# Linear attention and a bilinear FFN on one core: regrouped units, one more group by seven products, every step placed by a plan

## The chip, the core and the metric

The kernel runs on one core of a Trainium2 chip. The engines named here are TensorE (PE, matmuls; PEld its weight loads), VectorE (DVE), ScalarE (ACT), GpSimd (POOL) and SyncE (SP, which issues nearly all DMAs). Each takes its own instructions in order and waits on semaphores for the others. The metric is device microseconds of one execution, the median of several runs.

## The reference

q, k and v are (4 batches, 8 heads, 768 positions, 64), float32. The attention is linear with a decay lam per head. The result is transposed to x, 3,072 rows of 512, and goes through a bilinear FFN: w_a and w_b are 512 x 1,536, w_out is 1,536 x 512.

```python
for b in range(nb):
    intra = np.einsum('bhic,bhjc->bhij', qb, kb) * Dmask[None]
    intra = np.einsum('bhij,bhjd->bhid', intra, vb)
    inter = np.einsum('bhid,bhde->bhie', qb * lam_pow[None], kv_state)
    out[:, :, sl] = intra + inter
    kv_state = lam_block[None, :, None, None] * kv_state + np.einsum('bhsd,bhse->bhde', kb_dec, vb)
a = x @ w_a
b = x @ w_b
return (a * b @ w_out).astype(np.float32)
```

## The kernel before

Work is cut into 24 units: four batches of six blocks of 128 positions, all heads. `GROUPS` (line 28) joins units into groups of 4, 1, 2, 4, 4, 4, 4 and 1; the FFN runs on a group at a time, while the attention of later units is put between its matmuls.

Steps of one unit: q, k and v are loaded as float32 (`load_x`, line 181), q and k are scaled by powers of lam to bf16 (`make_ks`, `make_qs`, lines 406 and 411), v is cast (`make_vb`, 414), q and k are transposed (a DMA for units in `DMA_T`, else `piece_T` on TensorE, 438), scores are made (`scores`, 451, half the array at a time) and masked (`mask`, 465), the state is updated (`kv_update`, `kv_beside`, `kv_copy`, 535 to 560), and `pieces_O` (571) makes inter and intra products and evacuates them to xT. The first four units are loaded and transposed together (lines 336 to 352 and 874 to 1000).

The FFN of a group: `ffn` (646) makes a and b by plain matmuls over 512, multiplies them to ab and multiplies ab by w_out. The groups in `Z_GROUPS` (82) make a and b by `ffn_z` (714): the two-by-two block product is made by seven block products instead of eight (Strassen's scheme), from sums of weights (`weight_sum`, 260) and of xT (`x_sums`, 700). Each of the six column pairs n of ffn_z makes tiles U, V and W in PSUM, ScalarE snapshots (`snap`, 809), VectorE subtracts them into oab, a ring of two buffers, and multiplies oab to ab (line 738). Groups in `ZO_GROUPS` (83) do the product with w_out in seven products too: `ab_sum` (814) makes sums of ab, and `out_half` (835) runs 14 halves, placed into the next group. The other groups' out stage is plain.

What sets the order is written out in the source. `PLAN` (line 42) lists for each group pairs of slot and piece; the FFN functions call `hook(slot)` after each step, and the hook emits the pieces of that slot. Each engine then has the order of emission as its queue. Which engine takes a piece is in tables (`MASK_ACT`, `KV_ENG`, `VB_ENG`, `SUM_ENG`, `XS_ENG`, `WS_ENG`, `WO_ENG`, lines 87 to 110). Loads are not in the plan: `pump` (302) issues the next ones of a fixed list whenever a piece has freed a place, with all weights ahead of units 4 and later. The products of oab to ab are always VectorE's and come right behind the last of the seven products.

```python
    for g, n in enumerate(GROUPS):
        if g in Z_GROUPS:
            ffn_z(g, g_u0[g], gx.pop(g), hook, joined, own)
        else:
            ffn(g_u0[g], n, gx.pop(g), hook, g == 0, g + 1 == len(GROUPS))
```

Of the kernel before, what the change touches and what calls it, by code (L numbers as in the profile page):

```python
# [16 lines left out]
F32 = mybir.dt.float32  # L17
# [5 lines left out]
def _bc(ap, dims):  # L23
# [4 lines left out]
GROUPS = (4, 1, 2, 4, 4, 4, 4, 1)  # L28
W_CHUNKS = (256,) * 6
W_STEPS = ((0, 1), (2,), (3,), (4, 5))  # L30
W_HALVES = (4, 5)
LOOKAHEAD = {9: 2, 10: 1}
DMA_T = range(7, 24)
KEEP_GROUPS = 2
PACK = 4

PLAN = {
# [38 lines left out]
}  # L81
Z_GROUPS = (3, 4, 5, 6)
ZO_GROUPS = (4, 5, 6)
FIN_AT = 5
N_LATE = 3
# [28 lines left out]
def kernel(  # L114
# [116 lines left out]
    def cast_w(kind, c, eng):  # L231
        t, slot = staged.pop((kind, c))
        if slot is not once:
            slots.append(slot)
# [844 lines left out]
```

## Time and profile before

| what | value |
|---|---|
| median of 3 runs | 225.31 us (225.09 to 227.28) |
| span of the profiled execution | 224.7 us |
| granted TensorE clock | 1.000 over the span |
| TensorE busy | 214.6 us, 2,235 matmuls |
| VectorE busy | 164.8 us, 269 instructions |
| ScalarE busy | 123.2 us, 251 instructions |
| GpSimd busy | 101.1 us, 95 instructions |
| moved by DMA | 39.42 MB, mean 175 GB/s |

The profile is of one execution; its span goes from the first to the last instruction of the kernel. Busy time of an engine is the union of its instructions' times. A matmul's duration holds its way through the array, so neighbours overlap, and the rate of a stream is read from start to start, not from the mean duration. A name such as L730 is a line of the kernel; `op out<-in` names the tiles. "Idle before, releaser" is what an engine waited for.

### The profile page before, as it was taken

To read this page: it belongs to the slowest core of one execution; us is meant where nothing else is said; L and a number is where in the kernel's file an instruction comes from. 1 tells how busy PE (TensorE), PEld (TensorE's weight loads), DVE (VectorE), ACT (ScalarE), POOL (GpSimd) and SP (SyncE) were. 2 spreads that over 40 slices of the span, in tenths; PEclk is the share of its full clock that TensorE was granted. 3 is DMA by queue.
4 is the path that set the end of the run, shared out by engine and by line. 5 is a ranking of instruction groups with operands and counts; after the bars stand their busy time and mean duration, and the time that the engine had idled before them with its cause. 6 is when DMAs were issued, how large, how long until landed. Compare 5 with 4: busy or idle time off the path is not lost.

```text
span 224.7 us, 5609 instructions
## 1 busy us (share of the span) xinstructions
PE 214.6 (96%) x2235; PEld 158.8 (71%) x2235; DVE 164.8 (73%) x269; ACT 123.2 (55%) x251; POOL 101.1 (45%) x95
## 2 busy tenths in 40 slices
PE   7699999989989999999999999899999999999994
PEld 2375444437768757887547878688888888887994
DVE  1895673599699659989878999968686765777440
ACT  3586446017544247775366988776536665533322
POOL 6061004256895075541459359786417722052000
PEclk9999999999999999999999999999999999999999
DMA  4999999998999999999999999652021100112042
GB/s 137 316 231 356 356 384 346 276 217 192 229 198 218 219 180 240 204 253 247 175 240 243 243 206 202 138 98 48 2 88 55 50 1 4 47 48 95 0 143 93
DMA packets 99081, 39.42 MB, mean 175 GB/s; under 512 B 85488, under 2 KB 95088, under 8 KB 99056
## 3 DMA queue, kind: packets, MB, share of 16 engines
q1 hardware_dynamic: 98768, 39.00, 78.0%
q8 instruction: 17, 0.28, 0.5%
q10 hardware_dynamic: 288, 0.07, 0.1%
q14 instruction: 8, 0.07, 0.1%
HBM read 28.32 MB, written 6.29 MB: 154 GB/s over the span
## 4 chain that ended last, share of the span: by engine, by line
PE 80%; DVE 6%; DMA 6%; ACT 3%; issue 2%; SPq 1%; ACTq 0%; DVEq 0%
PE U L730 17%; PE op L852 12%; PE b_ps L596 9%; PE op L643 8%; PE V L730 8%; PE a_ps L596 8%; PE op L792 5%; PE W L730 4%; DMA wst<-in_moe_w_b_dram 4%; PE o_ps L497 3%; DMA k<-in_k_dram 3%; PE kq L457 2%; PE kvd L527 1%; SPq L350 1%; DVE m L480 1%
## 5 line engine op out<-in xcount | busy, mean ns | idle before, releaser
L811 ACT COPY u<-U 128x512 f32<-128x512 f32 x48 | 28.4, 591 | 16.9 <-PE U L730 16.6
L401 POOL TENSOR_TENSOR qk<-kf,lp_k 128x512 bf16<-128x512 f32 x18 | 19.8, 1099 | 34.6 <-DMA kf<-in_k_dram 23.1
L623 DVE TENSOR_TENSOR ab<-a_sb,b_ps 128x128 bf16<-128x128 bf16 (+2 forms) x48 | 19.2, 417 | 14.0 <-ACT a_sb L605 11.1
L480 DVE TENSOR_TENSOR m<-kq,lotri 128x512 bf16<-128x512 f32 x40 | 25.7, 684 | 3.8 <-PE kq L457 3.6
L596 PE MATMUL a_ps<-xT,wa_sb 128*128 128x128 bf16 (+2 forms) x200 | 27.8, 268 | 0.6 <-ACT xT L520 0.5
L596 PE MATMUL b_ps<-xT,wb_sb 128*128 128x128 bf16 (+2 forms) x192 | 27.5, 272 | 0.7 <-ACT oab L736 0.5
L738 DVE TENSOR_TENSOR ab<-oab 128x1024 bf16<-128x1024 bf16 x24 | 18.4, 767 | 10.5 <-ACT oab L736 10.5
L401 POOL TENSOR_TENSOR qk<-qf,lp_q 128x512 bf16<-128x512 f32 x20 | 25.2, 1259 | 1.2 <-DMA qf<-in_q_dram 1.2
L605 ACT CAST a_sb<-a_ps 128x128 bf16<-128x128 f32 (+2 forms) x48 | 17.1, 375 | 14.4 <-PE a_ps L596 14.3
L643 PE MATMUL op<-wo_sb,ab 128*128 128x512 bf16 (+2 forms) x120 | 22.8, 337 | 0.2 <-DVE wo_sb L254 0.2
L596 PEld LDWEIGHTS <-wa_sb 128*128 128x128 bf16 x200 | 16.6, 98 | 6.6 <-issue 0.7
L596 PEld LDWEIGHTS <-wb_sb 128*128 128x128 bf16 x192 | 15.7, 98 | 7.3 <-DVE wb_sb L251 0.7
L730 PEld LDWEIGHTS <-wz_a 128*128 128x128 bf16 x192 | 18.2, 98 | 3.6 <-issue 0.7
L730 PEld LDWEIGHTS <-wz_b 128*128 128x128 bf16 x192 | 18.7, 98 | 2.2
L730 PE MATMUL U<-xT,wz_a 128*128 128x256 bf16 x96 | 18.3, 272 | 0.0
L730 PE MATMUL U<-xT,wz_b 128*128 128x256 bf16 x96 | 18.3, 272 | 0.0
L520 ACT CAST xT<-o_ps 128x512 bf16<-128x512 f32 (+1 forms) x24 | 12.2, 556 | 10.7 <-PE o_ps L497 10.5
L420 POOL CAST vb<-vf 128x512 bf16<-128x512 f32 x14 | 10.9, 778 | 13.9 <-DMA vf<-in_v_dram 13.9
L769 DVE TENSOR_TENSOR oab<-U,u 128x512 bf16<-128x512 f32 x24 | 16.4, 682 | 0.4 <-PE U L730 0.4
L730 PEld LDWEIGHTS <-wa_sb 128*128 128x128 bf16 x144 | 13.4, 97 | 4.5 <-issue 1.7
L643 PEld LDWEIGHTS <-ab 128*128 128x128 bf16 x120 | 10.1, 98 | 8.6 <-issue 0.3
L736 ACT CAST oab<-U 128x512 bf16<-128x512 f32 x24 | 14.2, 591 | 3.6 <-PE U L730 3.5
(126 smaller groups left out, 453.8 us busy)
## 6 DMA issues: line engine op xcount, KB each, us to landing
vf<-in_v_dram SPq DMA_DIRECT2D x24, 256.0 KB, 4.8
qf<-in_q_dram SPq DMA_DIRECT2D x20, 256.0 KB, 4.6
kf<-in_k_dram SPq DMA_DIRECT2D x20, 256.0 KB, 4.6
out_dram<-o_sb SPq DMA_DIRECT2D x18, 256.0 KB, 2.5
wst<-in_moe_w_a_dram SPq DMA_DIRECT2D x6, 512.0 KB, 8.5
wst<-in_moe_w_b_dram SPq DMA_DIRECT2D x6, 512.0 KB, 9.0
wst<-in_moe_w_out_dram SPq DMA_DIRECT2D x6, 512.0 KB, 10.6
out_dram<-o_kept SPq DMA_DIRECT2D x5, 256.0 KB, 4.4
```

Source lines behind the costliest of these rows:

```text
L401: eng_of(eng).tensor_mul(dst.rearrange("p (c b) d -> p b c d", b=2), x[:].rearrange("p (b c) d -> p b c d", b=2), lp.rearrange("p (b c) o ...
L480: nc.vector.tensor_mul(m, kq[i], lotri_bc)
L596: nc.tensor.matmul(ps[:, lo:hi], lhsT=w_sb[:, s, f * 128:(f + 1) * 128], rhs=xT[:, s, lo:hi], start=(s == 0), stop=(s == KS - 1), skip_gro ...
L605: nc.scalar.copy(a_sb[:, :gt], ps[:, :gt])
L623: nc.vector.tensor_mul(ab[:, f, :gt], a_sb[:, :gt], ps[:, :gt])
L643: nc.tensor.matmul(op[:, lo:hi], lhsT=ab[:, f, t * 128:(t + 1) * 128], rhs=wo_sb[:, f, lo:hi], start=(f == 0), stop=(f == FC - 1))
L730: nc.tensor.matmul(ps[:, k, :], lhsT=wt[:, s, n * 128:(n + 1) * 128], rhs=rhs[i][:, s, :], start=(fresh and k == 0 and s == 0), stop=True, ...
L736: nc.scalar.copy(oab[:, 0], U)
L738: nc.vector.tensor_mul(ab[:].rearrange("p (h i) (t c) -> p h i t c", h=2, t=2)[:, :, n], o5[:, :, :, 0, :], o5[:, :, :, 1, :])
L769: nc.vector.tensor_sub(oab[:, 1], U, v1)
L811: nc.scalar.copy(t, ps)
L852: nc.tensor.matmul(ps[:, t, :], lhsT=lhs[p][:, n, t * 128:(t + 1) * 128], rhs=rhs[:, n, :], start=fresh, stop=True, skip_group_check=True)
```

## The change

The groups become 4, 1, 3, 4, 4, 4, 4. The group of three also goes by seven products, with tiles of 192 columns (hw, half a group's columns, in place of the fixed 256); its out stage is plain. The four groups of four all have their out stage by seven products. The plan now holds every step after the first scaling of q and k: loads (LQ, LK, LV, LW), casts of parts of a weight (CW), scaling (PK, PQ), casts of v (CV), transposes (TR), scores (S), masks (M), state (V, K), outputs of attention and their evacuation (O, E), sums (X, WS, WO, SM), out halves (H), products of oab (MU) and late stores (W). A table VAR names for each step which engine or form it takes. `pump` and its look-ahead are gone. All tiles that are loaded are float32, as before.

Three forms are new. Scores may be made in 64 x 64 quarters of the array, 16 matmuls instead of 8 (VAR of S); inter may use all 128 rows (VAR of O); products of oab may run on GpSimd (VAR of MU), which 13 of 30 do. Masks of a unit lie in one tile, so that one VectorE operation can mask both halves. The rows of the first four units that are kept for later stores lie in other tiles. In the built program TensorE has 2,327 matmuls instead of 2,235 and changes between whole, half and quarter array 87 times instead of 81; 16 transposes go by DMA instead of 17.

```diff
-GROUPS = (4, 1, 2, 4, 4, 4, 4, 1)
+GROUPS = (4, 1, 3, 4, 4, 4, 4)
+Z_GROUPS = (2, 3, 4, 5, 6)
+ZO_GROUPS = (3, 4, 5, 6)
...
 PLAN = {
...
+    5: [
+        (-1, 'X', (5, 1)), (-1, 'H', (3, 9)), (-1, 'PK', 22), (-1, 'LV', 21), (-1, 'V', 20),
+        (1, 'SM', (4, 0)), (1, 'SM', (4, 2)), (2, 'H', (3, 12)), (2, 'LQ', 22), (2, 'LV', 23),
...
+VAR = {('CV', 3): 2,
...
+  ('MU', (6, 0)): 1,
+  ('MU', (6, 1)): 1,
+  ('O', (5, 6)): 1,
+  ('PK', 4): 1,
...
+    def dve_pool(name, arg):
+        return nc.gpsimd if var(name, arg) else nc.vector
...
     def scores(u, kq=None):
         d = U[u]
         kq = kq or score_banks()
+        step = 64 if var("S", u) else 128
         for hp in range(HP):
-            for i in range(2):
-                p = slice(64 * i, 64 * i + 64)
-                nc.tensor.matmul(kq[i][:, hp, :], lhsT=d["kT"][p, hp, :], rhs=d["qT"][p, hp, :],
-                                 start=True, stop=True, skip_group_check=True)
+            for j in range(0, 128, step):
+                for i in range(2):
+                    p, r = slice(64 * i, 64 * i + 64), slice(j, j + step)
+                    nc.tensor.matmul(kq[i][r, hp, :], lhsT=d["kT"][p, hp, r], rhs=d["qT"][p, hp, :],
+                                     start=True, stop=True, skip_group_check=True)
...
+    def times(x):
+        g, n = x
+        hw = outs[g]["hw"]
+        o5 = oabs[x][:].rearrange("p (h t) k c -> p h t k c", h=2)
+        dve_pool("MU", x).tensor_mul(
+            outs[g]["ab"][:].rearrange("p (h i) x -> p h i x", h=2)[:, :, n, :2 * hw]
+            .rearrange("p h (t c) -> p h t c", t=2),
+            o5[:, :, :, 0, :], o5[:, :, :, 1, :])
...
         def last_product(n, U, oab):
             product(U, n, 2)
             nc.scalar.copy(oab[:, 0], U)
-            o5 = oab[:].rearrange("p (h t) k c -> p h t k c", h=2)
-            nc.vector.tensor_mul(
-                ab[:].rearrange("p (h i) (t c) -> p h i t c", h=2, t=2)[:, :, n],
-                o5[:, :, :, 0, :], o5[:, :, :, 1, :])
+            oabs[g, n] = oab
...
+        last = g + 1 == len(GROUPS) and i == 13
...
+        if last:
+            for t in range(T):
+                o = o_pool.tile([128, 256], F32, name="o_end", tag="osb")
+                nc.scalar.copy(o, ps[:, t, :])
+                (nc.scalar if t else nc.sync).dma_start(out=out_r[d["u0"] + t, :, :HN], in_=o)
+            return
...
+        hook, plan = hooks(g)
+        hook(-1)
         if g in Z_GROUPS:
-            bank["held"] = set(range(5))
-            joined = any(name == "H" and us[0] < g for slot, name, us in PLAN[g])
-            own = any(slot >= 18 for slot, name, us in PLAN[g])
-            ffn_z(g, g_u0[g], gx.pop(g), hook, joined, own)
+            hold(5)
+            ffn_z(g, g_u0[g], gx[g], hook, g - 1 in ZO_GROUPS,
+                  g not in ZO_GROUPS or g + 1 == len(GROUPS))
+        elif g:
+            hold(0)
+            ffn_plain(g_u0[g], n, gx[g], hook)
         else:
-            bank["held"] = {3, 4} if fin else set()
-            if fin:
-                fin.pop()()
-            ffn(g_u0[g], n, gx.pop(g), hook, g == 0, g + 1 == len(GROUPS))
+            ffn(g_u0[g], n, hook)
```

`ffn_plain` is the plain FFN of the group of one unit, with four column blocks to a PSUM tile; `plain_out` is a plain out stage that runs all units' early matmuls first and the last ones behind them.

More of the change, by code (lines that the diff above doesn't have):

```diff
@@ new lines, in dma_T, with make_vb @@
+    def dma_T(u):
+        qkT = qkT_pool.tile([128, 2, HP, 128], BF16, name="qkT", tag="qkT")
+        nc.sync.dma_start_transpose(
+            out=qkT[:].rearrange("p j hp i -> p (j hp) i"),
+            in_=U[u]["qk"][:].rearrange("p j h d -> p (j h d)"))
+        U[u]["qT"], U[u]["kT"] = qkT[:, 0], qkT[:, 1]
+    def make_vb(u):
+        vb = prep_pool.tile([128, H, D], BF16, name="vb", tag="vb", bufs=N_VB)
+        how = var("CV", u)
+        if how == 2:
+            nc.scalar.copy(vb, raw[u, "v"])
+        else:
+            (nc.vector if how else nc.gpsimd).tensor_copy(vb, raw[u, "v"])
+        raw[u, "v"] = vb
@@ L646, in ffn, with ffn_first @@
-    def ffn(u0, n, xT, hook, first, last):
+            nc.tensor.matmul(op, lhsT=ab[:, f, t * 128:(t + 1) * 128],
+                             rhs=wo_sb[:, f, :], start=(f == f0), stop=(f == f1))
+    f_ps, f_a = {}, {}
+    f_ab = []
+    def ffn_first(x):
+        kind, f, part = x
+        gt = n0 * BLK
+        lo, hi = ((0, gt // 2), (gt // 2, gt), (0, gt))[part]
+        ps_parts[0] = part < 2
+        k = kind, f
+        f_ps[k] = half(wa_sb if kind == "a" else wb_sb, f, gx[0], kind + "_ps", lo, hi, f_ps.get(k),
+                       {("a", 0): 0, ("a", 1): 3, ("b", 0): 4, ("b", 1): 5}[k] if part == 0 else None)
+        ps_parts[0] = False
+        if part == 0:
+            return
+        if kind == "a":
+            f_a[f] = a_copy(f_ps[k], gt)
+        else:
+            if not f_ab:
+                f_ab.append(ab_pool.tile([128, FC, 512], BF16, name="ab", tag="ab"))
+            nc.vector.tensor_mul(f_ab[0][:, f, :gt], f_a[f][:, :gt], f_ps[k][:, :gt])
@@ new lines, in ffn_plain, with plain_out @@
+        plain_out(u0, n, ab, hook, slot)
+    def plain_out(u0, n, ab, hook, slot, last=(FC - 1,)):
+        ops = [ps_bank("op", [128, d_model], F32, ffn=True) for _ in range(n)]
+        first = [f for f in range(FC) if f not in last]
+        for t in range(n):
+            out_mms(ops[t], ab, t, first, first[0], last[-1])
+            hook(slot)
+            slot += 1
+        for t in range(n):
+            out_mms(ops[t], ab, t, last, first[0], last[-1])
+            store(u0 + t, ops[t])
+            hook(slot)
+            slot += 1
@@ new lines, in mask4, with kv_part @@
+    def mask4(x):
+        i, up, par = x
+        how = var("M4", x)
+        if (i, up) not in ms4:
+            m = msk_pool.tile([128, H, 128], BF16, name="m", tag="m")
+            ms4[i, up] = [m[:, :HP], m[:, HP:]]
+        m, kq = ms4[i, up][par], kqs[i, up][par]
+        if how:
+            nc.scalar.copy(m, kq)
+            (nc.gpsimd if how == 2 else nc.vector).tensor_mul(m, m, lotri_bc)
+        else:
+            nc.vector.tensor_mul(m, kq, lotri_bc)
+    sts = {}
+    def kv_part(x):
+        u, hps, at = x
+        if u not in sts:
+            sts[u] = kv_bank() if at is None else ps_bank(f"kv{u}", [128, HP, 2, D], F32, at=at)
+        for w in range(u + 1):
+            kv_mms(sts[u], w, hps, w == 0)
```

748 lines of the change are left out of this document (298 added, 450 removed), and 290 rows, old and new, of tables (PLAN, VAR).

## The prediction

> **What bounds the kernel now.** I read the stretches of the span first, cut where the trace shows a stage begin, then the chain of waits, then the groups by form. The columns are the stretch, its length, and the busy time of each engine with its instructions.
>
> ```profile
> PE 214.6 (96%) x2235; PEld 158.8 (71%) x2235; DVE 164.8 (73%) x269; ACT 123.2 (55%) x251; POOL 101.1 (45%) x95
> ...
> PE 80%; DVE 6%; DMA 6%; ACT 3%; issue 2%; SPq 1%; ACTq 0%; DVEq 0%
> ```
>
> ```profile
> 0.00:18.20 18.20, 14.66 (x184) 8.62 (x185) 11.93 (x21) 10.47 (x19) 7.67 (x24) 1.00 0.86 238
> 18.20:53.20 35.00, 33.87 (x193) 16.10 (x194) 23.05 (x34) 14.88 (x25) 8.23 (x9) 1.00 1.05 310
> 53.20:84.70 31.50, 30.94 (x407) 23.33 (x405) 24.21 (x48) 15.23 (x39) 21.12 (x19) 1.00 1.19 208
> 84.70:118.70 34.00, 33.67 (x330) 23.64 (x329) 30.24 (x47) 20.40 (x40) 15.45 (x15) 1.00 1.27 229
> 118.70:143.10 24.40, 23.52 (x282) 18.90 (x281) 22.72 (x35) 20.06 (x40) 16.87 (x13) 1.00 1.06 205
> 143.10:175.20 32.10, 31.96 (x364) 27.13 (x364) 24.62 (x38) 20.12 (x41) 20.50 (x14) 1.00 0.30 69
> 175.20:203.70 28.50, 28.50 (x270) 24.91 (x269) 19.91 (x32) 15.51 (x30) 9.61 (x6) 1.00 0.12 39
> 203.70:224.70 21.00, 17.54 (x218) 16.14 (x216) 8.13 (x21) 6.55 (x20) 1.64 (x1) 1.00 0.23 76
> ```
>
> TensorE is nearly full in every stretch but the first and the last, and the chain runs over it for 80% of the span. VectorE is the close second from 84.7 to 143.1 (53 of 58 us). So the time is the stream of matmuls, plus the waits inside it, plus its two ends. The stream is priced from runs of equal matmuls in the chain:
>
> ```profile
> 32.67 3.45 PE a_ps L596 x16
> ...
> 87.47 0.54 PE V L730 x4
> ...
> 88.89 0.44 PE V L730 x4
> ```
>
> Sixteen of 512 columns take 3.45 us, 216 ns each; four of 256 columns take 0.44, 109 each. The same four take 0.54 when scores, which use half the array, stand just before or after them: a change of tile shape costs about 95 ns. Start to start over all neighbours of one shape, the trace gives 56 ns for 128 columns, 25 to 26 for the half-array matmuls of scores and intra, and 13 to 14 for the quarter-array ones and for the half-array ones of 64 columns.
>
> **The change part by part.** *The stream.* I counted the matmuls of both programs in their order. Before: 1,034 of 256 columns (113.0 us), 225 of 512 (48.7), 355 of 128 (20.0), 4 of 192 (0.3), 535 on part of the array (11.4), and 81 whose successor has another shape, at 129 to 311 ns each (14.3): 207.7 us. After: 1,027 of 256 (112.2), 186 of 512 (40.2), 224 of 128 (12.6), 166 of 192 (13.7), 636 on part of the array (12.1) and 87 at a change (14.4): 205.3. So the stream loses 2.4 us. Three more units go by seven products instead of eight, and one more group of four in its out stage; the six added changes of shape (0.6) and 101 more small matmuls take part of it back. The 192-column price, 82 ns, is the middle between 128 and 256 columns; two neighbours in the warm-up show 82, so I keep it.
>
> *The ends.* Before, the first matmul starts at 1.25 us, the last at 221.5, and the span ends at 224.7: 4.4 us. The new last step copies two tiles of 256 columns instead of one of 128 (ScalarE rows: 372 against 266 ns) and sends 128 KB instead of 64 (1.7 against 1.6 us): +0.2.
>
> *The waits.* Stage length less its part of the stream gives before's waits: 5.9 us up to 18.2 (after the 1.25), 1.8 to 53.2, 0.9 to 84.7, then 0.8, 1.5, 0.7 and 0.3 in the four seven-product stages, and 0.65 at the end: 12.6 in all. The same stages after:
>
> First products (18.2 before). Loads of q and k and their scaling are untouched, so the last transposes of k still start near 12.0 us. The half of the scores that before fills the time at 11.4 now stands behind them, so 6.3 us of stream follow, against 6.2 us of elapsed time before. That stream has loops TensorE, ScalarE, TensorE: the copy of k in its natural order (587 to 811 ns) is read 0.4 us of stream later, masks (682) one step later. Summed along the stream they cost 2.1. The weights don't hide this: the first chunk used lands one load later than 17.65, near 19, and is then cast. So the products start near 20.4: +1.9 after 0.3 to 0.4 of added stream. Bounds: 0.5 (if the loops overlap) to 3.5 (ScalarE's added copies also queue).
>
> The rest of the first group. Waits that go: 0.36 at 22.1 (weights cast) and 1.26 near 46 (scaling of unit 4 behind the weight sums). The new order of weights fits: 512 KB mostly lands 1.35 to 1.5 us after the last, so a chunk of both weights comes in 2.8 us, while its matmuls need 3.5. I take -1.3; bounds -1.8 and +1.
>
> Groups of one and three units. Before spends 30.6 us of stream and 0.9 of waits on units 4 to 6, of which 0.8 is one evacuation that nothing covers (64.2). After needs unit 7 too by about 65 us; 13 loads at 1.15 us and one of a weight bring its v to about 59, where before had it at 60.8. I take -0.4; bounds -0.9 and +3, the latter if the queue falls behind by three loads.
>
> Seven-product stages. By count times the median row of each form (for 192-column tiles, an estimate between the rows of 256 and 512 elements) VectorE has 25.6, 22.5, 27.8, 26.6, 20.4 us of work beside 27.3, 22.3, 29.2, 31.7, 28.2 of stream. Before's two full stages (VectorE 55.2 beside 56.1) lost 2.3 us, 4.1% of the stream, the two others 1.7%. With 4.1% of the first three (78.8) and 1.7% of the last two (59.9) the waits are 4.2 against 3.3: +0.9. Bounds: -2.0, if only the loops through a single evacuation stay (31 to 45 ns each), and +6.
>
> The end. One unit's own products go; the last group's out stage runs alone for 10.4 us, with two snapshots of 0.59 that leave 0.16 each uncovered (half a product lasts 0.66): -0.3, bounds -0.6 and +1.
>
> GpSimd: of the products of oab, all 24 VectorE's before, 13 of 30 now go to it, nine of full size. Against VectorE's row
>
> ```profile
> L738 DVE TENSOR_TENSOR ab<-oab x24: 676/692/1525, 91.3 to 204.6; 128x1024 bf16<-128x1024 bf16 x24
> ```
>
> GpSimd's three bf16 sums of that size took 2.1 to 2.6 us. I cost this at nothing beyond the 0.9: the oab ring has two buffers and a pair of products lasts 5.3 us, so a product may be 2.5 us late. If that cover is gone, it is the second rival.
>
> ScalarE (100.5 us of rows beside 138.7) and the DMA queues (the same loads, one transpose fewer) are costed at nothing: both run ahead, the loads until buffers of q, k and v (three each) are full. A load issued late on SyncE, which is in order and now follows the plan, holds all behind it; that is the +3 above.
>
> Waits sum to +1.9 -1.3 -0.4 +0.9 -0.3 = +0.8. With -2.4 and +0.2 the span is 224.7 - 1.4 = 223.3. The runs' median stands 0.6 above the profiled span, so 223.9 us.
>
> **The rivals.** *Waits vanish.* After the head only short loops stay (0.4 in the 192-column group, about 1 elsewhere): waits of 7.8 + 0.2 + 1.4 = 9.4, so 205.3 + 4.6 + 9.4 = 219.3, measured 219.9. For it: before's largest waits after 53 us (0.8, 0.5, 1.0, 0.66) are each one step whose producer stood too late, and each can be had for a move. Against: VectorE at 90% and more in three stages leaves little to move.
>
> *GpSimd becomes a link.* In the seven-product stages its rows sum to 80.9 us where before had 56.6. Its queue is in order: a product stands behind scalings of q and k (1.04 each, up to 1.79), the ring fills, and VectorE's next write of oab waits with the masks and subtractions behind it. If each of the nine full-size products is late by one scaling, 1.04, that is 9.4 us, 5.2 more than the 4.2 counted: 229.1. It makes the kernel over 1% slower from 0.9 us each. For it: GpSimd pays 1.64 for a sum that VectorE makes in 0.55. Against: its rows fill only 58% of those stages.
>
> *VectorE and GpSimd slow each other.* Twenty VectorE operations in the trace took over 0.1 us more than the shortest of their form, each with GpSimd busy for at least half of it; from 80 us on that is 7.4 us beside 62 us of GpSimd, 0.12 per us. With 27 us more of GpSimd VectorE grows by 3.2: 227.1 if all of it reaches TensorE. The Trainium skill, "GPSIMD Engine Reference", Specifications, says that the two share their SBUF interfaces and contend when VectorE reads two SBUF inputs; the trace agrees, since the 692 ns product above reaches 1,525, and by that rule the change would pay the 3.2. Against its full price: VectorE has 10% of these stages free.
>
> *The change does not do what it says* (the seven products aren't fewer matmuls) is excluded by the counts.
>
> **How the numbers follow.** Forecast 0.38, vanishing waits 0.26, GpSimd a link 0.22, mutual slowing 0.10, something else 0.04. The forecast's own range is 221.5 to 226, its bounds not all falling on one side. About 1% (223.06 and 227.56) is what a measurement of this kernel can tell from no change. Faster: 0.14 of the forecast, 0.25 of the first rival, 0.02: 0.41. Slower: 0.19 of the second, 0.03 of the third, 0.02: 0.24. Within: 0.35. The range 218.5 to 229.5 takes in both outer rivals' middles and leaves out the ends of each.
>
> **What would show it.** Stream: again 3.45 us for 16 matmuls of 512 columns, 0.33 for four of 192, and a sum of 205. Head: the first a_ps near 20.4 us instead of 18.16, the waits before it on ScalarE's scratch. Seven-product stages of 28.3, 23.2, 30.4, 32.2 and 28.7 us. If GpSimd is the link, VectorE's oab rows wait for GpSimd's ab, and TensorE for VectorE, in spans over 1 us; if mutual slowing, VectorE's bf16 means rise with no such waits. I am wrong in the mechanism if the stream's sum does not fall by about 2.4, or if waits after 55 us exceed 10.

## The result and the profile after

| | us, median | ratio of after to before |
|---|---|---|
| before (20 runs) | 225.97 | |
| after (20 runs) | 228.28 | 1.0089, 95% interval 1.0063 to 1.0116 |

A median is of all runs of a kernel; a ratio leaves out runs more than 1.5% above that kernel's fastest. The kernel became 0.9% slower; 223.9 us, 0.6% faster, had been forecast. The profiled execution after has a span of 226.7 us, before 224.7, both at a granted clock of 1.00. First the page of the kernel after, its busy times and the shares of its chain of waits:

```profile
PE 214.4 (95%) x2327; PEld 162.1 (72%) x2327; DVE 168.8 (74%) x266; ACT 131.5 (58%) x261; POOL 116.2 (51%) x106
...
PE 74%; DMA 13%; DVE 6%; SPq 3%; issue 2%; POOL 1%; ACT 0%; DVEq 0%
```

TensorE is as busy as before, with 92 more matmuls. VectorE gained 4 us of work, ScalarE 8, GpSimd 15. The stretches of the span of the kernel after, cut where a stage's first product starts (same columns as in the prediction):

```profile
0.00:20.82 20.82, 16.03 (x187) 9.22 (x188) 10.80 (x18) 12.99 (x25) 7.82 (x23) 1.00 0.94 257
20.82:56.54 35.72, 34.87 (x221) 17.49 (x214) 23.68 (x36) 18.00 (x33) 17.06 (x18) 1.00 0.98 286
56.54:67.34 10.80, 10.80 (x203) 8.62 (x201) 9.21 (x17) 7.03 (x15) 2.93 (x3) 1.00 0.91 193
67.34:96.84 29.50, 28.38 (x362) 21.34 (x360) 22.97 (x42) 18.37 (x42) 17.48 (x15) 1.00 0.98 196
96.84:119.35 22.51, 22.51 (x305) 18.49 (x301) 20.85 (x33) 17.25 (x34) 14.60 (x12) 1.00 1.16 242
119.35:149.64 30.29, 29.90 (x355) 24.89 (x349) 27.73 (x42) 21.10 (x44) 20.75 (x15) 1.00 0.70 137
149.64:182.95 33.31, 32.06 (x365) 27.37 (x363) 26.24 (x41) 18.34 (x36) 20.71 (x14) 1.00 0.44 96
182.95:226.70 43.75, 39.84 (x360) 34.71 (x357) 27.29 (x43) 18.44 (x35) 14.89 (x8) 1.00 0.20 67
```

The first column is a stretch's length. Set against the stream of matmuls that I had counted for each stage, priced from start to start, it gives the waits (the parts and the 1.25 us ahead of the first matmul sum to the span):

| part | before, us | forecast | after |
|---|---|---|---|
| stream of matmuls | 207.7 | 205.3 | 205.3 |
| waits up to the first product | 5.8 | 7.7 | 8.06 |
| rest of the first group | 1.89 | 0.5 | 1.87 |
| plain groups (1 and 3 units before, 1 after) | 0.95 | 0.5 | 0 |
| five seven-product stages (four before) | 3.3 | 4.2 | 5.7 |
| last out stage | 0.6 | 0.3 | 0.4 |
| last matmul's start to the end | 3.15 | 3.35 | 4.12 |

The prices of the stream came out as forecast. In the chain of the kernel after, 16 matmuls of 128 columns take 0.89 us (56 ns each), four of 256 columns 0.44, and 0.54 beside a change of tile shape:

```profile
57.59 0.89 PE b_ps L832 x16
...
96.91 0.54 PE U L916 x4
97.45 0.44 PE V L916 x4
```

So 2.4 us of matmuls went, 3.5 us of waits ahead of the last matmul and 1.0 behind it came. The two largest waits behind 57 us are of different kinds. In the timeline of the kernel after (start, length, engine, line, tiles; in brackets the idle time before and what ended it) the first is this:

```profile
82.50 1.04 POOL L562 TENSOR_TENSOR qk<-kf,lp_k 128x512 bf16<-128x512 f32 x1
83.50 3.24 POOL L887 TENSOR_TENSOR ab<-oab 128x768 bf16<-128x768 bf16 x2
85.18 0.56 DVE L941 TENSOR_TENSOR oab<-W,u 128x384 bf16<-128x384 f32 x1 [2.18 <-POOL ab L887]
85.65 0.68 DVE L685 CAST xT<-o_ps 128x512 bf16<-128x512 f32 x1
86.39 0.40 PE L615 MATMUL kq<-qkT 64*128 64x128 bf16 x8 [1.12 <-DVE xT L685]
```

GpSimd makes two products behind a scaling of k. The inputs of the first were complete at 81.12 (ScalarE's copy), but ahead of it in GpSimd's queue stood a cast of v, which waited 1.70 us for its load, and that scaling. VectorE wants to write the next oab, whose buffer the first of them still reads, and idles 2.18 us; its copy of transposed x stands behind that, and the scores behind the copy: 1.12 us of TensorE. This is the full ring of the second rival. The other, from the same view:

```profile
177.44 2.12 POOL L871 TENSOR_TENSOR z_sub<-xT 128x1024 bf16<-128x1024 bf16 x1
...
177.61 2.51 DVE L887 TENSOR_TENSOR ab<-oab 128x1024 bf16<-128x1024 bf16 x1 [1.08 <-ACT oab L922]
...
180.04 0.68 DVE L1047 TENSOR_TENSOR o_sb<-op,u 128x512 f32<-128x512 f32 x1
...
180.77 0.81 PE L1028 MATMUL op<-wy,ab 128*128 128x256 bf16 x6 [1.25 <-DVE o_sb L1047]
```

A product that takes 0.69 us elsewhere starts 0.17 us into a GpSimd difference and takes 2.51. It ends at 180.12, 0.56 after GpSimd did; the subtraction behind it, which frees PSUM for TensorE, comes too late by 1.25 us. That is the third rival's mechanism, in one place.

### The profile page after: what moved, and what is told of

The parts are those of the page before. It is cut to its first block, busy times and chain, and to the rows that moved or that the text cites. A ratio compares the mean times of both kernels' runs of the same rounds, so it can differ in the third digit from the quotient of the medians.

```text
span 226.7 us, 5761 instructions
## 1 busy us (share of the span) xinstructions
PE 214.4 (95%) x2327; PEld 162.1 (72%) x2327; DVE 168.8 (74%) x266; ACT 131.5 (58%) x261; POOL 116.2 (51%) x106
## 4 chain that ended last, share of the span: by engine, by line
PE 74%; DMA 13%; DVE 6%; SPq 3%; issue 2%; POOL 1%; ACT 0%; DVEq 0%
PE U L916 22%; PE op L1028 15%; PE V L916 11%; PE op L784 7%; PE W L916 6%; DMA wst<-in_moe_w_a_dram 4%; PE o_ps L654 3%; DMA wst<-in_moe_w_out_dram 3%; PE kq L615 3%; SPq L438 3%; DMA k<-in_k_dram 3%; PE b_ps L751 2%; DMA lam_sb<-in_lam_dram 2%; PE a_ps L751 2%; PE a_ps L832 1%
## 5 line engine op out<-in xcount | busy, mean ns | idle before, releaser
L978 ACT COPY u<-U 128x512 f32<-128x512 f32 (+1 forms) x60 | 34.3, 571 | 35.3 <-PE U L916 33.2
L887 POOL TENSOR_TENSOR ab<-oab 128x1024 bf16<-128x1024 bf16 (+1 forms) x13 | 26.4, 2041 | 10.3 <-ACT oab L922 8.8
L784 PE MATMUL op<-wo_sb,ab 128*128 128x512 bf16 x96 | 22.9, 379 | 0.2 <-DVE wo_sb L448 0.2
L956 DVE TENSOR_TENSOR oab<-U,u 128x512 bf16<-128x512 f32 (+1 forms) x30 | 19.7, 657 | 3.7 <-PE U L916 3.6
L916 PE MATMUL U<-xT,wz_a 128*128 128x256 bf16 (+1 forms) x120 | 22.3, 267 | 0.0
L916 PE MATMUL U<-xT,wz_b 128*128 128x256 bf16 (+1 forms) x120 | 22.2, 267 | 0.0
L1028 PEld LDWEIGHTS <-ab 128*128 128x128 bf16 x192 | 18.6, 98 | 3.8 <-issue 1.4
L953 DVE TENSOR_TENSOR oab<-V,u 128x512 bf16<-128x512 f32 x18 | 12.4, 688 | 11.8 <-PE V L916 10.9
L1028 PE MATMUL op<-wy,ab 128*128 128x256 bf16 x144 | 18.7, 273 | 1.2 <-DVE o_sb L1047 1.2
L922 ACT CAST oab<-U 128x512 bf16<-128x512 f32 (+1 forms) x30 | 17.1, 571 | 3.9 <-PE U L916 3.9
L978 ACT COPY u<-V 128x512 f32<-128x512 f32 (+1 forms) x30 | 17.3, 575 | 1.2 <-PE V L916 1.1
L784 PEld LDWEIGHTS <-ab 128*128 128x128 bf16 x96 | 9.0, 98 | 10.4 <-issue 0.5
```

Source lines behind the costliest of these rows:

```text
L784: nc.tensor.matmul(op, lhsT=ab[:, f, t * 128:(t + 1) * 128], rhs=wo_sb[:, f, :], start=(f == f0), stop=(f == f1))
L887: dve_pool("MU", x).tensor_mul(outs[g]["ab"][:].rearrange("p (h i) x -> p h i x", h=2)[:, :, n, :2 * hw] .rearrange("p h (t c) -> p h t c" ...
L916: nc.tensor.matmul(ps[:, k, :], lhsT=wt[:, s, n * 128:(n + 1) * 128], rhs=rhs(i)[:, s, :], start=(fresh and k == 0 and s == 0), stop=True, ...
L922: nc.scalar.copy(oab[:, 0], U)
L953: nc.vector.tensor_sub(oab[:, 3], X, u2)
L956: nc.vector.tensor_sub(oab[:, 1], U, v1)
```

## The experiments

Ratios are to the kernel before, measured in the same batch; the kernel after stands at 1.0089.

| run | us, median | ratio and interval |
|---|---|---|
| e1 all products behind their copies, on VectorE | 239.46 | 1.0544 (1.0500 to 1.0588) |
| e9 the same place, engines of after | 245.67 | 1.0846 (1.0789 to 1.0903) |
| e17 ten products back on VectorE, places of after | 235.52 | 1.0389 (1.0347 to 1.0430) |
| e2 one product earlier | 227.53 | 1.0040 (1.0016 to 1.0063) |
| e3 two sums to VectorE | 228.07 | 1.0011 (0.9972 to 1.0050) |
| e4 scores ahead | 227.60 | 1.0069 (1.0033 to 1.0106) |
| e5 scores ahead, loads reordered | 231.95 | 1.0197 (1.0140 to 1.0254) |
| e6 three single waits | 228.43 | 1.0067 (1.0014 to 1.0120) |
| e8 all six sums to VectorE | 229.52 | 1.0110 (1.0065 to 1.0155) |
| e10 GpSimd's products left out | 228.70 | 1.0090 (1.0051 to 1.0129) |
| e11 GpSimd's sums of x left out | 227.82 | 1.0047 (1.0013 to 1.0081) |
| e12 both left out | 226.20 | 0.9995 (0.9965 to 1.0026) |
| e13 VectorE's products left out | 228.30 | 1.0083 (1.0049 to 1.0118) |
| e14 e2, e3 and e4 together | 226.13 | 0.9998 (0.9974 to 1.0022) |
| e15 e14 and one more sum on VectorE | 226.47 | 1.0014 (0.9991 to 1.0036) |
| e18 e14 and three head steps moved | 227.63 | 1.0051 (1.0017 to 1.0086) |
| e19 e18 and a weight sum later | 226.56 | 0.9997 (0.9967 to 1.0027) |
| e20 e14 and one sum before its neighbour | 226.27 | 0.9993 (0.9964 to 1.0021) |

### Is it the engine of the products, or their place?

e1, all 30 products on VectorE right behind ScalarE's copy, as in the kernel before:

```diff
-        (11, 'MU', (2, 0)), (14, 'PQ', 9), (14, 'TR', 9), (15, 'MU', (2, 1)), (15, 'LK', 13),
+        (14, 'PQ', 9), (14, 'TR', 9), (15, 'LK', 13),
...
             nc.scalar.copy(oab[:, 0], U)
             oabs[g, n] = oab
+            nc_times(nc.vector, (g, n))
```

> All 30 products of oab go back to VectorE, right behind ScalarE's last copy, as in the kernel before; the rest of the changed kernel stays. GpSimd theory (its late products and its contention with VectorE make the waits of the seven-product stages): the wait of 1.19 us near 86 us and the one of 1.41 us near 181 us go, waits of the five seven-product stages fall from 5.7 us (2.23, 0.61, 1.07, 1.60, 0.2) to about 3.3, and the span falls from 226.7 to about 224.3. VectorE theory (it is full in these stages, so what is taken off GpSimd comes back as VectorE's time): 13 products of 0.55 to 0.69 us come to it, 8.4 us, and the waits stay at 5.7 or grow, span 226.7 to 230.

It cost 11 us against the kernel after, more than either reading had allowed for, and looked like the price of 13 products on VectorE. But the run changed engine and place together. e9 keeps that place and gives each product its engine of the kernel after:

```diff
-            nc_times(nc.vector, (g, n))
+            nc_times(nc.gpsimd if VAR.get(("MU", (g, n))) else nc.vector, (g, n))
```

> The products keep their engines of the kernel after (13 on GpSimd, 17 on VectorE) but leave their planned slots: each stands right behind its ScalarE copy in issue order, as in the run with all of them on VectorE. It tells the engine from the place. If the engine was what that run showed (13 products of about 0.9 us more on VectorE's list): within 2 us of the kernel after, 227 to 230 us. If the place was it (a product right behind its copy holds VectorE's list until the copy is done): close to that run's 239.5 us, 236 us or more.

245.67 us: worse still. So with the engines of the kernel after the place alone costs 17 us: a product that stands in an in-order queue right behind the copy it needs holds all the rest of that queue. GpSimd waits 17.1 us for ScalarE's copies in its profile (8.8 in the kernel after), VectorE 7.6 (2.3). In the kernel before, all products stand in that place at 226 us, so it is dear in this plan and not everywhere. Some 3.4 us of this profile are lost where the granted clock was 0.50 (last section). e17 is the engine alone, at the planned places, for the ten products where that is possible:

```diff
-  ('MU', (2, 1)): 1,
-  ('MU', (2, 2)): 1,
...
-  ('MU', (5, 5)): 1,
```

> Ten of GpSimd's 13 products go back to VectorE at their planned slots (the other three would wait there for one another), nothing else changes: the engine alone, where the two runs with all products behind their copies changed the place too. If taking products off VectorE is what the change lives on there: some 9 us of work come back to VectorE and the stage waits grow, 230 us or more. If VectorE has the room and the products on GpSimd cost as much by coming late (about 2.0 us each there against 0.95) and by holding VectorE: 226.3 to 228.5 us.

235.52 us, which fits the first of the two readings, yet the profile says otherwise. Its span is 231.3, a time of 233.05 us, the shortest of the six. There four of the five seven-product stages wait about as long as after (0.4, 1.3, 2.1 and 0.6 us against 0.6, 1.1, 1.6 and 0.6, the last with the out stage behind it); the group of three waits 6.9 instead of 2.2. In the timeline of e17:

```profile
84.42 0.56 DVE L931 TENSOR_TENSOR oab<-W,u 128x384 bf16<-128x384 f32 x1 [3.83 <-POOL ab L877]
...
85.04 0.33 PE L906 MATMUL W<-z_add,wa_sb 128*128 128x192 bf16 x2 [2.31 <-DVE oab L931]
...
86.90 0.33 PE L906 MATMUL U<-z_sub,wa_sb 128*128 128x192 bf16 x2 [1.04 <-DVE oab L946]
```

VectorE idles 3.83 us for the one product of that group that stayed on GpSimd: the full ring again. Of the 4.6 us that this stage lost, 1.6 are not waits: from 87.8 to 91.2 us the granted clock was 0.50, and matmuls of 192 columns started 0.16 us apart instead of 0.08. So the price of the engine as such stays unmeasured; in this execution the ring is the dearer part of it. What the other 2.5 us of the median are no trace shows; all six executions have a clock below 1.00 (0.984 to 0.993).

### Single waits taken away

e2 puts that fourth product of the group of three seven slots earlier; e3 gives two sums of the last group's x, the z_sub and z_mix of the lines above, to VectorE; e4 puts the first half's scores and masks ahead.

```diff
-(35, 'MU', (2, 3)),
+(28, 'MU', (2, 3)),
```
```diff
-  ('X', (6, 0)): 1,
-  ('X', (6, 2)): 1}
```
```diff
-        (0, 'LV', 1), (0, 'TK', (1, 1, 2)), (0, 'NK', ((0, 1, 2), (0, 1), 3)),
+        (0, 'LV', 1), (0, 'S4', (0, 0, (5, 6))), (0, 'M4', (0, 0, 0)), (0, 'M4', (0, 0, 1)),
+        (0, 'S4', (0, 1, (0, 1))), (0, 'M4', (0, 1, 0)), (0, 'M4', (0, 1, 1)), (0, 'TK', (1, 1, 2)),
...
-        (0, 'S4', (0, 0, (5, 6))), (0, 'M4', (0, 0, 0)), (0, 'M4', (0, 0, 1)), (0, 'K4', 2),
+        (0, 'K4', 2),
...
```

> One product of oab (fourth pair of the group of three) stays on GpSimd but stands ahead of the scaling of k of unit 13 in its queue, where it stood behind it. GpSimd theory: the wait of 1.19 us of the scores near 86 us goes, and the waits of that stage fall from 2.23 to about 1.0; span 225.5. VectorE theory: VectorE's idle time of 2.18 us there goes, but the stage gains less than 0.5 us, since VectorE is behind at its end anyway.

> Two sums of xT for the last group (z_sub of 128x1024 and z_mix of 128x512) go from GpSimd to VectorE. GpSimd theory: the product of oab beside them takes 0.69 us in place of 2.51, the wait of 1.41 us near 181 us goes, and the span falls to about 225.3, VectorE's added 1.1 us lying in its free time (84% of that stage). VectorE theory: the added 1.1 us appears as a wait of the same stage, span 226.4 to 227.

> In the head the scores and masks of the first four heads stand ahead of the last transposes of k again, as before. Head theory (ScalarE's and VectorE's loops behind the late scores cost the 2.3 us by which the first products start later): first a_ps near 19.0 to 20.0 us instead of 20.82, and the span falls by 0.8 to 1.8. Rival (weights: the first chunk used lands near 18.8 and GpSimd casts it until 19.96): first a_ps not before 20.0, or the gain is given back as a wait for wb_sb or wa_sb between 21 and 25 us, span down by less than 0.5.

e2: the wait near 86 is gone, and 0.5%. But its stage still waits 1.8 us instead of 2.2, for there is a new wait of 0.7 at 82: beside the moved product a mask of VectorE took 1.48 instead of 0.41. In later runs with this edit the stage waits 1.9 to 2.9, in e14 5.4. So it is not shown that the 0.5% comes from this wait. e3: the wait near 181 is gone. The difference is now VectorE's own and is held itself (1.59 us, beside GpSimd's z_add); the product takes its usual time:

```profile
180.26 1.59 DVE L870 TENSOR_TENSOR z_sub<-xT 128x1024 bf16<-128x1024 bf16 x1
181.77 0.68 DVE L886 TENSOR_TENSOR ab<-oab 128x1024 bf16<-128x1024 bf16 x1
```

The stage waits 0.19 us instead of 1.60, here and in all five later runs with this edit. The ratio fell by 0.8%, the median of all its runs by 0.2% only. e4: the first product still started at 20.81 us; 0.2% went, inside the interval. Its first group waited 0.8 instead of 1.9, which is inside the scatter of that stage (0.4 to 2.3). New waits stand at 118 to 120 in the profiles of e2 and e3 (2.0 to 2.4 us) and at 61 in that of e3 (2.1, for a transpose by DMA). e6 took three at once: e2's edit, the weight sum `WS 2` behind the projection copy that it held (0.7 us at 56), and one of the two last copies on VectorE:

```diff
-(21, 'WS', 2),
...
+(22, 'PQ', 7), (22, 'WS', 2),
...
-                nc.scalar.copy(o, ps[:, t, :])
+                (nc.vector.tensor_copy if t else nc.scalar.copy)(o, ps[:, t, :])
```

> Three single waits of the kernel after taken away at once, nothing of the arithmetic changed: the fourth product of the group of three goes seven slots earlier on GpSimd's list (wait of 1.19 us at 86), one weight sum on VectorE goes behind the projection copy that it held (0.71 us at 56), and the second of the two last copies goes to VectorE, beside the first on ScalarE (0.35 us at the end). Theory (each wait is path time): -2.2 us against the kernel after, about 226.0 us, no wait over 0.5 us near 56 and 86, and the last store issued some 0.35 us earlier after the last matmul. Rival (the executions scatter, and a gap that closes is opened again by the next VectorE operation that meets GpSimd): the waits at 56 and 86 are gone in the profile but others over 1 us stand at 115 to 120 or at 177 to 181, and the time falls by less than 1 us, to 227.3 us or more.

The rival's picture: the waits at 56 and 86 are gone, others stand at 77 (1.0), 83 (0.7), 119 (2.1) and 182 (1.4), and the median is that of the kernel after. The one at 77 comes from a cast of v on VectorE that took 1.73 us instead of 0.42 beside a GpSimd product. The end didn't shrink either: VectorE's copy started only when ScalarE's was over (idle 1.02 us for it), and the time from the last matmul's start is 4.0 instead of 4.1.

e8 moved all six of GpSimd's sums of transposed x to VectorE:

```diff
-  ('X', (4, 0)): 1,
...
-  ('X', (6, 2)): 1}
```

> All sums and differences of transposed x go to VectorE, six of them from GpSimd, whose two-input work in the group stages then is products and loaded-x sums alone. Theory (VectorE operations with both inputs in SBUF are held beside GpSimd's z_sub, z_add and z_mix: 0.55 us became 2.47, 0.69 became 2.51): no wait over 1 us at 115 to 121 and at 177 to 183, and the runs scatter less than the 226.6 to 231.8 of the kernel after; time about 227 us. Rival (VectorE is the scarce engine there, as when all products came back to it: six sums of 0.55 to 0.7 us, about 3.6 us of work): the waits are replaced by VectorE queueing in front of the same groups' first matmuls, and the time is 228.5 us or more.

229.52 us, the rival's time again; by the ratio no difference from the kernel after. Moving work off GpSimd wholesale doesn't pay.

### What GpSimd's reading costs

In e10 to e13 operations are replaced by fills of the same bytes:

```diff
+        if VAR.get(("MU", x)):
+            dve_pool("MU", x).memset(
...
-            eng.tensor_sub(d[0], xT[:, :, lo], xT[:, :, hi])
+            eng.memset(d[0], 0.5) if eng is nc.gpsimd else eng.tensor_sub(d[0], xT[:, :, lo], xT[:, :, hi])
```

> In GpSimd's 13 products of the seven-product groups the multiplication is left out: the same bytes are filled with a constant at the same places, nothing is read. VectorE's 17 products stay. If GpSimd's products are what the waits of the five stages (5.7 us over the floor in the profile after, 4.2 forecast) come from, by holding VectorE and by coming late themselves, 1.5 to 3 us go and the time is 225.3 to 226.8 us; the wait of 1.19 us at 86 goes in any case. If the stalls come from GpSimd's sums of transposed x, the waits of 1 to 2 us near 117 to 121 and 177 to 183 stay and the time is above 227.3 us.

> GpSimd's six sums and differences of transposed x (z_sub, z_add, z_mix of groups 4 to 6) are left out: the same bytes are filled with a constant, nothing is read; the products stay on their engines. If VectorE is held beside these sums (0.55 us became 2.47, 0.69 became 2.51), the waits of 1 to 2 us near 117 to 121 and 177 to 183 are gone, the stage waits of groups 4 to 6 fall by 1.5 to 2 us, and the time is 226.3 to 227 us; when the same six sums were on VectorE it was 229.5, so what they cost there as work would be the difference. If the products are at fault, the time stays within 0.7 us of the kernel after (227.6 to 228.9).

> Both at once: GpSimd reads nothing for products or for sums of transposed x in the seven-product stages. It gives the whole of what GpSimd's two-input work costs there. Theory (GpSimd, by its lateness and by holding VectorE, is what the forecast missed in these stages): stage waits of the five fall from 5.7 to 2.5 to 3.5 us and the time to 225 to 226 us, with runs that scatter less. Rival (the waits come from VectorE's own load and from ScalarE's copies, whatever GpSimd does): above 227.3 us.

> The counterpart: VectorE's 17 products are replaced by fills at the same places, GpSimd's 13 stay. VectorE loses some 16 us of work of 169 (page: 17 products, 16.2 us) less what the fills take. If VectorE's own work is the bound of the stages, more than when GpSimd's products go: 224.5 to 226 us. If GpSimd's work is what counts: within 1 us of the kernel after, 227.3 us or more.

With products alone nothing went (the stalls at 119 and 182 stayed, 2.3 and 1.4 us); with the sums alone 0.4%, at the edge of the noise (the stages of groups 4 to 6 wait 0.8 us less, not 1.5 to 2); with both 0.9%, down to the kernel before. The profile of e12 has 4.5 us of waits in the seven-product stages and the last out stage together (6.1 after; forecast 4.2 and 0.3). Its span, 223.8, is lower by another 1.4 us because the first group, whose program is the same, waited 0.4 instead of 1.9. So GpSimd's reads cost about what the forecast missed in these stages, and by the medians only products and sums together. That is not the price of the change alone: five such sums of transposed x ran on GpSimd in the kernel before too, and that kernel was not run without them. The groups of e12, against a mean of 968 ns for the same 15 products of VectorE in the kernel after:

```profile
L892 DVE TENSOR_TENSOR ab<-oab 128x1024 bf16<-128x1024 bf16 x15 | 11.4, 771 | 2.0 <-ACT oab L927 2.0
```

e13 tells little: a fill on VectorE takes 887 ns on average and a product 960, so hardly any work was taken away, and the time stayed.

### Who starts first

In the timeline of the kernel after, around the stage that shows no wait there:

```profile
116.21 0.55 DVE L997 TENSOR_TENSOR zab<-ab 128x768 bf16<-128x768 bf16 x1
116.30 2.44 POOL L871 TENSOR_TENSOR z_sub<-xT 128x1024 bf16<-128x1024 bf16 x1 [0.56 <-ACT xT L683]
```

The same two operations in e6:

```profile
115.95 2.34 POOL L871 TENSOR_TENSOR z_sub<-xT 128x1024 bf16<-128x1024 bf16 x1 [0.19 <-ACT xT L683]
...
116.23 2.48 DVE L997 TENSOR_TENSOR zab<-ab 128x768 bf16<-128x768 bf16 x1
118.63 0.68 DVE L956 TENSOR_TENSOR oab<-U,u 128x512 bf16<-128x512 f32 x1
...
119.36 0.38 PE L916 MATMUL U<-z_sub,wa_sb 128*128 128x256 bf16 x2 [1.96 <-DVE oab L956]
```

Where VectorE began 0.09 us ahead, its sum took 0.55; where it began 0.28 behind, 2.48, and TensorE waited 1.96. Besides e20, fourteen profiles have this pair as it is here: in the six where zab began first (by 0.1 to 0.9 us) it took 0.55, in seven where z_sub did (by 0.2 to 0.5), 2.47 or 2.48. One, e13, is an exception: zab began 0.2 us after z_sub and took 0.49. There z_sub took 2.67, its shortest 2.12 and 0.55 more, behind a fill that VectorE was still making; so z_sub seems to have been the one held.

e14 makes the edits of e2, e3 and e4 together, e15 also gives this z_sub to VectorE (`('X', (4, 0))`), and e20 instead emits the sum ahead of the product it followed, about 1 us sooner:

```diff
-(27, 'MU', (3, 3)), (28, 'SM', (3, 0)),
+(27, 'SM', (3, 0)), (27, 'MU', (3, 3)),
```

> Three edits that each gained a little alone against the kernel after are made together: the fourth product of the group of three seven slots earlier, two sums of the last group's transposed x on VectorE, and the first half's scores and masks ahead of the keys' turn. If the lost time is a number of single meetings that placing takes away one by one, the gains add (0.5, 0.4 and 0.2 per cent of 226): -2.4 us against the kernel after, 225.9 us, level with the kernel before. If it is the whole of GpSimd's two-input work, which one placing only moves from one VectorE operation to the next: 227.0 to 228.0 us, and a wait over 1 us stands somewhere new.

> The same three edits and the difference of group 4's transposed x (z_sub, beside which VectorE's zab took 2.47 us instead of 0.55 in several profiles, with a wait of 2 to 2.4 us at 117 to 121) on VectorE too. If the meetings can be placed away: no wait over 0.7 us between 110 and 125, and 0.5 to 1 us less than without this edit, 225 to 226.5 us, perhaps below the kernel before. If not: no gain against it, or a loss of 0.5 us (z_sub is some 0.7 to 1.3 us of work on VectorE), and the wait turns up at another group.

> The three edits, and one VectorE operation more is moved: the sum zab of group 3 goes ahead of the product it followed (it needs only the three products before that one), so that it starts about 1 us earlier. In twelve profiles so far, whenever zab started before GpSimd's z_sub it took 0.55 us, and whenever z_sub had begun 0.2 to 0.5 us before it, 2.47, with a wait of 2.0 to 2.4 us of TensorE at 117 to 123. Theory (the later of two such operations waits for the earlier one, and a margin of about 1 us in place of 0.1 to 0.4 decides it): zab takes 0.55 us, no wait over 0.7 us between 110 and 126, the runs reach less far up than the 229 to 234 us of the three edits alone, and the median falls to 225.2 to 225.9, level with or up to 0.5 us below the kernel before. Rival (another VectorE operation, the product, then stands beside z_sub and is held instead): the same wait of 2 us in the profile or in the upper runs, and 226.0 to 226.8 us.

Alone the three edits of e14 gave 0.5, 0.8 and 0.2% (the expectation had counted 0.4 for the second), together 0.9%: they add up in part, to the level of the kernel before. That fits single meetings which placing takes back. In e15 and e20 the wait at 117 to 123 is gone from the profile (0.5 us left in e15), but neither median fell: the expected 0.5 us more didn't come, and the runs of e20 still reach up to 232.75 us (e14: 233.89). What this wait costs in the median is therefore open. The timeline of e20 shows the pair apart:

```profile
114.32 0.69 DVE L997 TENSOR_TENSOR zab<-ab 128x768 bf16<-128x768 bf16 x1
...
115.24 2.37 POOL L871 TENSOR_TENSOR z_sub<-xT 128x1024 bf16<-128x1024 bf16 x1 [0.64 <-ACT xT L683]
```

### The head

e5 took e4's order and put the loads of v3 and of the weight quarters in the order of their casts; e18 (on e14) moved v3's cast and one weight cast to VectorE and its copy of x ahead of a weight cast; e19 added e6's later weight sum.

```diff
-        (0, 'K4', 1), (0, 'LW', ('a', 1, 'O0')), (0, 'S4', (1, 1, (6, 0))), (0, 'CV', 2), (0, 'LV', 3),
-        (0, 'LW', ('a', 0, 'X')), (0, 'LW', ('b', 1, 'A0')), (0, 'LW', ('b', 0, 'O1')),
+        (0, 'K4', 1), (0, 'LV', 3), (0, 'LW', ('a', 0, 'X')), (0, 'S4', (1, 1, (6, 0))), (0, 'CV', 2),
+        (0, 'LW', ('a', 1, 'O0')), (0, 'LW', ('b', 0, 'O1')), (0, 'LW', ('b', 1, 'A0')),
```
```diff
-VAR = {('CV', 3): 2,
+VAR = {('CV', 3): 1,
...
-  ('CW', ('a', 0, 0, 3, 0, 128)): 1,
```

> Besides putting the first half's score and mask steps ahead (as in the run before), the loads of the first weight quarters are put behind one another in the order in which the casts on GpSimd use them, with the state's v3 ahead of them. Theory (the head's extra wait is the order of landing: v3 at 17.2 to 18.0 us and the first quarter at 19.64 hold the state copy and the first cast): the first group's first matmul starts at 18.5 to 19.0 instead of 20.8 us and the time falls by about 2 us against the kernel after, to some 226 us. Rival (only the amount of loads counts, all the bytes ahead of it must land anyway): the start stays at 20.5 to 20.8 and the time at 227.5 to 228.3; or the wait comes back inside the first group, whose 0.8 to 1.9 us then grow by the same 2 us.

> On top of the three edits: in the head, the cast of v3 goes from ScalarE to VectorE, which stands idle from 17.0 to 21.2 us there, one of the two first-quarter casts goes from GpSimd to VectorE, and VectorE copies its transposed x ahead of a weight cast that waits for its load. Theory (after the first quarter lands at 19.7 us, 1.1 us of casts on GpSimd and the state chain on ScalarE set the start): the first group's first matmul at 20.2 to 20.4 instead of 20.9 to 21.1 us, no second wait at 22 to 25, and 225.2 to 225.8 us, 0.3 to 0.8 below the kernel before. Rival (the loads bound the head: what starts earlier waits for the next quarter): start earlier, but the first group waits as much longer, 226.0 to 226.6 us.

> The same, and the weight sum that stood ahead of a projection copy on VectorE (a wait of 0.5 to 0.8 us at 55 to 57 in several profiles) goes behind it. If single meetings add up, as they did in the run of three edits: 0.3 to 0.5 us below the run without it. If the wait only moves to the next projection copy (0.42 us at 61.5 was seen in the run of small edits): no difference beyond 0.3 us.

The first product started at 20.88 in e5 and at 20.94 in e18, though GpSimd's part of the first quarter was cast by 19.99 and 20.16. So its load does not set the start. In e5 a wait came inside the group instead; its timeline (span 234.9, the longest of its six):

```profile
23.41 0.43 DVE L449 CAST wb_sb<-wst 128x512 bf16<-128x512 f32 x1 [2.58 <-DMA wst<-in_moe_w_b_dram]
...
23.76 0.68 DVE L686 CAST xT<-o_ps 128x512 bf16<-128x512 f32 x1
...
24.49 0.38 PE L752 MATMUL a_ps<-xT,wa_sb 128*128 128x256 bf16 x2 [2.29 <-DVE xT L686]
```

VectorE waited 2.58 us for a quarter of w_b, now loaded later, with the copy of x behind it. What stands ahead of the start in all these runs is the chain state on TensorE, its cast on ScalarE, outputs on TensorE, copy on ScalarE; that it sets the start is argued, not shown by a run that shortens it. e19 started at 20.4 and is level with the kernel before; e18 alone isn't, and is even 0.5% above e14, for which no trace gives a reason. The head of e19 is the same as that of e18, so the 0.5 us between their starts is scatter.

No version beat the kernel before beyond its interval. The best (e14, e19, e20) beat the kernel after by 0.9 to 1.0%.

## Why the prediction was wrong

- **Stream, -2.4.** Right: -2.4, at the forecast prices.
- **First products at 20.4, +1.9.** Right in size: 20.82, +2.3. The reason is half borne out, and so the number is partly luck. The last waits ahead of the products are for masks of the late scores, as I had it (0.42 and 0.67 us at 17.5 and 18.8). But in e4, where these scores stand ahead again, the start is 20.81 all the same: there the outputs wait 0.94 us for ScalarE's cast of the state, a loop that I had not named as the bound.
- **Rest of the first group, -1.3.** Wrong, 0.0 in the profile. The old waits went; new ones came: 0.7 us at 56, where a weight sum of VectorE took 1.79 instead of 0.95 beside a GpSimd scaling, and 0.4 us at 36.7 behind a cast of w_out. In the eleven profiles whose programs are the same up to there the group waited 0.4 to 2.3 us, median 1.2, so about half of this miss is this one execution's.
- **Plain groups, -0.4.** Nearly: -0.95, no wait left.
- **Seven-product stages, +0.9.** This is the step that failed: I took these waits as the same share of the stream as before (4.1 and 1.7%), and costed what GpSimd adds "at nothing beyond the 0.9". Measured +2.4, the largest part of the miss (1.5 of the 3.4 us in the span). Two single waits, the full ring's (1.2) and the held product's (1.4), are more than that together. The second is shown by its going (1.60 to 0.19 in six profiles); when the first went, others came, and its price stays open. Leaving out GpSimd's products alone gained nothing (e10), so the price is that of products and sums together. The cover that I named, a product 2.5 us late, was used up by one: at 86 it began 2.4 us after its inputs were complete, behind a cast and a scaling, and ran for 1.6.
- **Ends, +0.2.** Mis-sized: +1.0. Both last copies start only behind the last matmul, from one PSUM tile, and run one after the other on ScalarE (0.70 us; before one of 0.27): the last store is issued 1.04 us after the last matmul's start instead of 0.60. The other 0.5 lies behind that issue; the landing is 0.2 of it (1.8 against 1.6 us), the rest is open. I had priced one copy and one transfer.
- **0.6 us from span to median.** Also off: 1.6. In the executions listed with their spans the time is 1.7 to 1.8 us above the span, so before's span of 224.7 belongs to a time of about 226.4, not to 225.31. Of the 4.4 us between forecast and result, 3.4 are in the span and 1.0 is this.
- **Waits vanish, 219.9.** Not so: 6.1 us of waits stand behind the first group, where this rival had 1.4.
- **GpSimd a link, 229.1.** VectorE waits for a GpSimd product three times in the profile (3.3 us), and TensorE behind it once over 1 us, not nine times.
- **Mutual slowing, 227.1.** The nearest by the span (226.5 by this rival, measured 226.7; by the median, 228.28, the link is nearer), for a reason other than mine. I took 0.12 us of VectorE per us of GpSimd, and 3.2 us in all. The excess of all VectorE operations over the shortest of their tiles and form did not grow over the whole span, 12.8 us before and 12.4 after; from 80 us on it grew from 7.8 to 9.7, by 1.9. What counts is the single case: each is all or nothing, and costs when TensorE's next product hangs on it. e3 shows it for one case by taking the wait away.

## What to carry to other kernels

When work is given to a second engine, its duration is not the price: price the moment at which its result is read, with all that stands ahead of it in its queue, and what waits in the consumer's queue behind that. Where two engines can hold one another, a mean slowdown is no estimate; list the pairs that may overlap and ask which starts first and by what margin. Moving one of a pair makes it meet another operation (e2, e6), so look for the new pair too. A margin larger than the scatter took one wait out of e20's profile, but its median did not fall. Change place and engine of an operation in separate runs, for here the place alone (17 us, e9) was worth more than the engine with all that followed from it (7 us, e17).

## What the hardware showed

A VectorE operation with both inputs in SBUF that starts while GpSimd works on SBUF inputs doesn't slow down, it waits: it ends a fixed time after GpSimd ends. For the product of 128x1024, which takes 0.68 us alone, that is 0.55 us (in 96 of 106 cases over all profiles; the others up to 0.66), beside z_sub, z_mix, sums of ab or scalings of q and k alike; for sums of 128x768, 0.55 alone, 0.41 to 0.42. Subtractions and masks that read PSUM took their usual 0.54 to 0.69 us beside the same GpSimd operations. The Trainium skill, "SBUF — State Buffer", "SBUF: two separate sides", says that whichever of two such operations starts first holds the shared ports for the whole instruction and the other blocks fully; these traces agree. Beside GpSimd's fills, which read nothing, VectorE's products were not held so: they took 0.77 us on average in e12 and 0.97 after. Two inputs are not needed: VectorE's casts from SBUF to SBUF are held too. The cast of v of 128x512, 0.42 us alone, took 1.4 to 1.8 us beside GpSimd's work in e6, e18, e19 and e20, and TensorE then waited 1.0 us at 75 to 78.

The same program is not the same timing: with identical instructions up to 56 us, the first product started at 20.8 to 21.3 us and the first group waited 0.4 to 2.3 us from one execution to the next. Whether that decides which of two operations 60 us later comes first is not shown.

A wait of TensorE can cost twice. In seven of the twenty profiles the granted clock is 0.50 for 3.4 us (twice in e9 and e14, once for 6.8), beginning in a wait or up to 1.3 us behind it; matmuls of 256 columns then start 213 ns apart instead of 109, and some 1.6 us are lost each time. Not every such wait is followed by it: the profiles of e3, e6 and e19 have waits of 2 us at a clock of 1.00.
